# Pooling part of the second batch's pixels on GpSimd, and seventeen GELU chunks on VectorE

## The chip, the cores and the metric

The kernel runs on one core of one Trainium2 chip. A core has TensorE (PE in the profile; its weight loads are PEld), ScalarE (ACT), VectorE (DVE), GpSimd (POOL), SyncE (SP), and 16 DMA engines that all queues share. The metric is the device time of one execution in microseconds, lower is better; a few executions are taken and their median counts.

## The reference, cut to what matters

```python
# q: (4, 12288, 128)   kv: (4, 384, 32, 128)   w_sr: (128, 128)
kv_pool = kv.reshape(B, H // 4, 4, W // 4, 4, C).mean(axis=(2, 4))   # 96 x 8 pooled pixels
k = v = kv_pool.reshape(B, -1, C) @ w_sr                             # 768 keys for each batch
a = softmax(q @ k.T / sqrt(C));  x = (a @ v).reshape(B * S, D)       # 49152 x 128
h = x @ w_in;  out = (h / (1 + exp(-1.702 * h))) @ w_out             # w_in 128 x 2048, w_out 2048 x 128
```

Each batch's pixels are averaged over 4x4 blocks, projected to 768 keys that are also the values, and attended to by 12288 queries. The attention output goes through a two-layer network with a hidden width of 2048 and the quick GELU.

## The kernel before, in words

Queries are cut into 96 groups of 512, 24 to a batch; keys into six chunks of 128 (`JC`), the hidden width into 16 chunks of 128 (`FCH`). There are two rounds: attention of groups 0 to 47, their network, attention of groups 48 to 95, their network.

The unit of work is a **pass** of up to three chunks (`K = 3`). PE writes three 128x512 products into three PSUM banks (`fill_attn` at L347: keys times queries; `fill_moe` at L593: `w_in` times x), and one ACT instruction of 1536 columns takes exp (L349) or the GELU (L595) of them into a slot of `ag`. Two sets of three banks take turns, so PE fills one set while ACT reads the other. The first 30 passes are of one or two chunks. Later PE **drains** the slots: in attention twelve matmuls of 129 columns for three chunks (L360; the 129th column gives the sum for the division), in the network one matmul of 512 columns a chunk (L603). DVE divides (L383, L386) or transposes the result for the store (L614). `ag` has 102 slots, so that drains can lag behind fills.

Each engine executes its list in order. The lists are written by a **planner** in the kernel's Python (the loop at L794): it keeps a clock `now` in units of one 512-column matmul, believes ACT's pass to last `FIXED + CHUNK * 3` units, believes side jobs to last what `COST`, `COPY` and `RECIPROCAL` say, and decides which drain or side job goes on PE's list between two fills. Nothing of it runs on the chip: it changes only the order.

Some of ACT's work is done by DVE in about fifteen instructions a chunk: exp chunks (`early_exp`, from L428) and GELU chunks, the 16th chunk of chosen groups (`lent_gelu`, from L450, with two reciprocals at L470; its product is at L406). `lent` at L329 lists 14 of these: one in every third group from 52 on. The tile `aside` takes the results, three at a time.

**Pixels and keys.** Batches 0 and 1 are loaded in six chunks of 128 image rows by 16 pixels, cast to bf16 by the DMA that GpSimd issues (`load_chunk`, L130), into tiles of `x` that are not yet used. `pool_chunk` (L139) sums with 16 matmuls of 32 columns: the 128x32 matrix `sum4` adds four rows, four accumulated matmuls add four columns. DVE copies the pooled chunk (L142), and `key_and_value` (L161, L162) makes keys and values with two matmuls and two DVE copies. Batch 1's six loads are issued when the groups 10 and 12 begin, its jobs go into a list `extras` from group 15 on, one chunk a group; its keys are needed at group 24. Batches 2 and 3 are pooled by DMA accumulation and are not touched.

**Queries** beyond the first twelve groups are cast into `q_bf` in DRAM by GpSimd's queue (`cast_q`, L209) and come back transposed on SP's queue (`load_qT`, L215). `gate` (L517, L518) makes GpSimd's queue wait until DVE has come to a point of its list. `put_away` and `bring_back` (L500, L506) transpose the attention output through DRAM.

Of the kernel before, what the change touches and what calls it, by code (L numbers as in the profile page):

```python
# [7 lines left out]
F32 = mybir.dt.float32  # L8
F32R = mybir.dt.float32r
I32 = mybir.dt.int32  # L10
BF = mybir.dt.bfloat16
AF = mybir.ActivationFunctionType
AX = mybir.AxisListType
ADD = mybir.AluOpType.add
# [10 lines left out]
def kernel(  # L25
    ctx, tc, q, kv, w_sr, moe_w_in, moe_w_out, out,
):
    nc = tc.nc
    B, N, C = q.shape
    _, H, W, _ = kv.shape  # L30
    r = 4
    Hp, Wp = H // r, W // r
    J = Hp * Wp
    JC = J // 128
    d_ff = moe_w_in.shape[1]
    FCH = d_ff // 128
    scale = 1.0 / (C ** 0.5)
    G = 512
    SG = 4 * G
    NG = B * N // G  # L40
    NS = NG // 4
    GB = NG // B
# [10 lines left out]
    kv_r = kv.rearrange("b (ch p) (a w) c -> b a ch p (w c)", p=128, a=2)  # L53
# [6 lines left out]
    XS = NS // R  # L60
# [7 lines left out]
    kvtmp = ctx.enter_context(tc.tile_pool(name="kvtmp", bufs=1))  # L68
# [3 lines left out]
    opool = ctx.enter_context(tc.tile_pool(name="op", bufs=3))  # L72
# [8 lines left out]
    free = {2: 0.0, 5: 0.0, 6: 0.0, 7: 0.0}  # L81
    turns = [7, 6, 5]
    last_acc = 7

    def acc(key=None):

        nonlocal last_acc
        last_acc = next_acc()
        turns.append(last_acc)
        turns.remove(last_acc)  # L90
        if key:
            closes[last_acc] = key
        return banks[:, last_acc, :]

    def next_acc():
        return min((m for m in turns if m not in closes), key=lambda m: (max(free[m], now), turns.index(m)))
# [10 lines left out]
    now = 0.0  # L107

    x = xpool.tile([128, XS * SG], BF, name="x")
# [6 lines left out]
    HC = H // 128  # L116
    h = J // 2
    kv_tiles, kv_sums, pooled, pTs, kTs, vs = {}, {}, {}, {}, {}, {}

    def new_keys(b):  # L120
        kTs[b] = kvres.tile([128, J], BF, name="kT")

        vs[b] = kvres.tile([128, JC, C + 8], BF, name="v")
        nc.vector.memset(vs[b][:, :, C:C + 1], 1.0)

    def load_chunk(b, jc):

        a, ch = divmod(jc, HC)
        t = x_tile(XS - 1 - jc)
        nc.gpsimd.dma_start(out=t, in_=kv_r[b, a, ch])  # L130
        kv_tiles[b, jc] = t.rearrange("p (wp w1 c) -> p w1 wp c", w1=r, c=C)

    def pool_chunk(b, jc):
# [7 lines left out]
        pTs[b, jc] = kvtmp.tile([128, 128], BF, name="pTc", bufs=2)  # L141
        nc.vector.tensor_copy(pTs[b, jc], ps[:, 0:128])  # L142

    def key_chunk(b, jc):
        if jc == 0:
            new_keys(b)
        ps = acc()
        nc.tensor.matmul(ps[:, 0:128], w_sr_sb, pTs[b, jc], start=True, stop=True)
        nc.vector.tensor_copy(kTs[b][:, jc * 128:jc * 128 + 128], ps[:, 0:128])
# [5 lines left out]
        vs[b, jc] = True  # L155

    def key_and_value(b, jc):
        if (b, jc) == (1, 0):
            new_keys(b)
        ps = acc()  # L160
        nc.tensor.matmul(ps[:, 0:128], w_sr_sb, pTs[b, jc], start=True, stop=True)  # L161
        nc.tensor.matmul(ps[:, 128:256], pTs.pop((b, jc)), w_sr_sb, start=True, stop=True)  # L162
        nc.vector.tensor_copy(kTs[b][:, jc * 128:jc * 128 + 128], ps[:, 0:128])  # L163
        nc.vector.tensor_copy(vs[b][:, jc, 0:C], ps[:, 128:256])
        vs[b, jc] = True
# [52 lines left out]
    QS = 3  # L218
    qs = [x_tile(XS - 1 - JC - s) for s in range(QS)]

    def load_q(s, lo, hi):
        nc.gpsimd.dma_start(  # L222
            out=qs[s].rearrange("p (g e) -> p g e", g=4)[:, lo:hi, :],
            in_=q_flat[s * SG + lo * G:s * SG + hi * G, :].rearrange("(g p i) c -> p g (i c)", p=128, i=4))
# [22 lines left out]
    load_chunk(0, 1)  # L247
    load_q(0, 2, 4)
    load_q(1, 0, 2)
    for jc in range(2, JC):  # L250
        load_chunk(0, jc)
    load_q(1, 2, 4)
    for s in range(2, QS):
        load_q(s, 0, 2)
        load_q(s, 2, 4)
    cast_q(3)
    cast_q(4)

# [11 lines left out]
    for m in range(0, 128, 32):  # L270
        p = slice(m, m + 32)
        nc.vector.tensor_tensor(ident[p, p], row[p], col[p], EQ)
    sum4 = cpool.tile([128, 32], BF)
# [11 lines left out]
    w_sr_sb = cpool.tile([128, C], BF)  # L285
# [19 lines left out]
    parts = ag[:, 0:2 * SPLIT, :].rearrange("p (u a) t -> p u (a t)", a=2).bitcast(F32)  # L305
# [20 lines left out]

    early = range(NG // R, NG // R + EARLY)
    rolling = [(i, JC - 1) for i in [*range(38, NG // R, 6), *range(57, 90, 6)]]
    lent = [(g, FCH - 1) for g in range(52, 94, 3)]  # L329
    aside = agpool.tile([128, K, 512], BF, name="aside")  # L330

    def weights(c):
# [161 lines left out]
    PART, FIRST = 24, 3  # L494

    def put_away(n, m):
        size = PART // 2 if n == 0 and m > FIRST + 1 else PART
        for o in range(m * PART, m * PART + PART, size):
            lo = n * XS * SG + o * T
            nc.sync.dma_start(out=x_bf[lo:lo + size * T, :].rearrange("(k p) c -> p k c", p=T),  # L500
                              in_=x[:, o * T:(o + size) * T].rearrange("p (k c) -> p k c", k=size))
# [22 lines left out]
    def background(i):  # L524

        first_round = i < GB * 2
        s = TURN.get(i, NS) if first_round else i // 4 + 3 if i % 4 == 0 else NS
        if s < NS:
            load_qT(s)
        if i in CAST:  # L530
            gate()
            for s in CAST[i]:
                cast_q(s)
        if i in (10, 12):
            gate()
            for jc in range(i % 10 * 3 // 2, i % 10 * 3 // 2 + 3):
                load_chunk(1, jc)
        if 0 <= i - 16 < JC:
            extras.append((key_and_value, 1, i - 16))
        if 0 <= i - 15 < JC:  # L540
            extras.append((pool_chunk, 1, i - 15))
        if i in (28, 33, 38):
            put_away(0, (i - 28) // 5)
        if i in (31, 36, 41):
            bring_back(0, (i - 31) // 5)
        if i == 27:
            gate()
            nc.gpsimd.dma_start(out=w_in_sb, in_=moe_w_in)
        if i == 28:
            gate()  # L550
            nc.gpsimd.dma_start(out=w_out_sb, in_=moe_w_out.rearrange("(o p) c -> p o c", p=128))
# [34 lines left out]
    extras = []  # L586
# [67 lines left out]
    for n in range(R):  # L654
        part = [c for c in chunks if c[0] // (NG // R) == n]
        while part:
            m = sizes.pop(0) if sizes else K
            seq.append(("a", part[:m]))
            part = part[m:]
# [34 lines left out]
    def later(g):  # L694
        extras.append((transpose_q, g))

    def jobs(p):

        nonlocal now
        for f, *args in first.get(p, ()):  # L700
            if f in COST:
                now = max(now, free[next_acc()])
            f(*args)
            if f in COST:
                now += COST[f][0]
                free[last_acc] = copied(f)

    def prepare(p):

        nonlocal now  # L710
        kind, part = seq[p]
        for i, jc in part:
            if (kind, i) not in begun:
                begun.add((kind, i))
                (background if kind == "a" else background_moe)(i)
            while kind == "a" and ((key_and_value, i // GB, jc) in extras or (transpose_q, i) in extras):
                f, *args = extras.pop(0)
                now = max(now, free[next_acc()]) + COST[f][0]
                f(*args)
                free[last_acc] = copied(f)  # L720

    first = {
        0: [(pool_chunk, 0, 0), (transpose_q, 0), (warm, 1), (key_chunk, 0, 0), (transpose_q, 1)],
        1: [(value_chunk, 0, 0), (warm, 1)],
        2: [(pool_chunk, 0, 1), (warm, 2), (key_and_value, 0, 1), (warm, 1), (transpose_q, 2)],
        3: [(transpose_q, 3)],
        4: [(transpose_q, 4)],
        5: [(transpose_q, 5)],
# [6 lines left out]
        15: [(pool_chunk, 0, 5)],  # L735
        16: [(key_and_value, 0, 5), (later, 6)],
        17: [(later, 7)],
        18: [(later, g) for g in range(8, 12)]}

    FIXED, CHUNK, SWITCH, HANDOVER, EVACUATE = 0.295, 1.978, 6.0, 1.0, 4.5
    COST = {pool_chunk: (1.9, 2.6), key_chunk: (0.3, 2.4), value_chunk: (0.3, 2.4),
            transpose_q: (1.05, 4.2), early_fill: (1.0, 5.5), key_and_value: (0.55, 3.5),
            transpose_pooled: (0.9, 3.6), make_k: (0.8, 3.2), make_v: (0.8, 3.7)}
    COPY = {pool_chunk: 1.5, key_chunk: 1.5, value_chunk: 1.5, key_and_value: 2.8, transpose_q: 3.2}
    SMALL = 0.26
    RECIPROCAL = 10.5
    PAUSE = 4.0  # L750
    end, extra_at = [], 0.0
    source, dve = None, 0.0
# [7 lines left out]
    def copied(f):  # L760
        if f not in COPY:
            return now + COST[f][1]
        on_dve(COPY[f])
        return max(now + COST[f][1], dve)

    def fill(p):
        nonlocal now
        if p >= len(seq):
            return
        kind, part = seq[p]  # L770
        prepare(p)
        if p == 4:
            turns.insert(0, 2)
        if p == narrow - 5:
            for m in (2, 5):
                turns.remove(m)
        if p == narrow:
            assert not any(m in closes for m in (2, 5))
            now = max(now, free.pop(2), free.pop(5))
        lo = K * (p % 2)  # L780
        (fill_attn if kind == "a" else fill_moe)(part, banks[:, lo:lo + len(part), :])
        if p >= 2:
            now = max(now, end[p - 2] + HANDOVER / 2)
        now += len(part)
        begin = max(now + HANDOVER / 2, end[p - 1] if p else 0.0)
        if p and kind != seq[p - 1][0]:
            begin += SWITCH
        end.append(begin + FIXED + CHUNK * len(part))
# [101 lines left out]
```

The softmax here doesn't subtract the row's maximum and nothing guards it: scores larger than these inputs give would overflow.

## Time and profile before

| what | value |
|---|---|
| device time, median of 3 | 950.07 us (949.90 to 951.19) |
| span of the profiled execution | 948.6 us |
| PE busy | 941.8 us, 6314 matmuls |
| ACT busy | 934.9 us, 710 instructions |
| DVE busy | 536.5 us |
| GpSimd busy | 66.5 us |
| ACT passes of 1536 columns | 664 (502 GELU, 162 exp) |
| attention, first round | to 141.9 us |
| network, first round | to 487.3 us |
| attention, second round | to 604.3 us |
| network, second round | to the end |

An engine that is busy all the time need not be the one that sets the time: a matmul's record runs from its start to its modelled end, and matmuls overlap, so the starts of successive matmuls tell more than the busy share. ACT's instructions overlap too (1507 ns in the records of L595, while a new one starts about every 1340 ns).

### The profile page before, as it was taken

How to read it: one execution, taken by the hardware profiler on the slowest of the kernel's cores; microseconds unless marked ns; L12 is line 12 of the kernel's file. 1: busy time of each engine (PE TensorE's matmuls, PEld its weight loads, DVE VectorE, ACT ScalarE, POOL GpSimd, SP SyncE). 2: the span in 40 equal slices, each digit the busy share in tenths (PEclk: the TensorE clock that was granted, in tenths of full speed). 3: DMA queues.
4: the chain of work that ended last, by engine and by line, in shares of the span. 5: the costliest groups of instructions: out<-in, count | busy, mean ns of one | idle time of the engine just before them, and what ended most of it. 6: DMA issues, size and time to landing. Idle time of an engine off the chain costs nothing.

```text
span 948.6 us, 15423 instructions
## 1 busy us (share of the span) xinstructions
PE 941.8 (99%) x6314; PEld 502.9 (53%) x6314; DVE 536.5 (57%) x1035; ACT 934.9 (99%) x710; POOL 66.5 (7%) x114
## 2 busy tenths in 40 slices
PE   8999999999999999999999999999999999999998
PEld 4677776444444444454446777754444444444444
DVE  4643653102577777778655765365666665566631
ACT  6999999999999999999999999999999999999998
POOL 3101001320000232000000000000000000000000
PEclk9999999999999999999999999999999999999999
DMA  9999922999767799864335583562222222222222
GB/s 209 209 170 193 206 64 45 158 125 180 153 130 115 113 154 119 123 103 79 64 55 113 134 161 76 133 122 36 43 35 44 34 46 34 45 33 45 34 45 45
DMA packets 372855, 95.46 MB, mean 101 GB/s; under 512 B 346720, under 2 KB 370400, under 8 KB 372320
## 3 DMA queue, kind: packets, MB, share of 16 engines
q1 hardware_dynamic: 344000, 62.36, 36.9%
q0 software_dynamic: 28512, 31.99, 22.3%
q8 instruction: 49, 0.80, 0.4%
q14 instruction: 22, 0.18, 0.1%
q10 hardware_dynamic: 272, 0.13, 0.0%
HBM read 52.49 MB, written 48.76 MB: 107 GB/s over the span
## 4 chain that ended last, share of the span: by engine, by line
ACT 88%; PE 9%; DMA 2%; issue 0%; DVE 0%; POOL 0%; POOLq 0%
ACT ag L595 71%; ACT ag L349 17%; PE banks L347 4%; PE banks L360 3%; DMA qT<-q_bf 1%; DMA x<-in_kv_dram 1%; PE banks L139 0%; PE banks L593 0%; PE banks L631 0%; ACT L595 0%; PE banks L603 0%; PE banks L233 0%; ACT L349 0%; DVE kT L163 0%; POOL x L222 0%
## 5 line engine op out<-in xcount | busy, mean ns | idle before, releaser
L595 ACT ACTIVATE ag<-banks 128x1536 bf16<-128x1536 f32 (+1 forms) x510 | 682.2, 1507 | 0.0
L593 PE MATMUL banks<-x,w_in_sb 128*128 128x512 bf16 x1522 | 411.7, 379 | 0.1
L603 PE MATMUL banks<-ag,w_out_sb 128*128 128x512 bf16 x1506 | 407.8, 379 | 0.0
L349 ACT ACTIVATE ag<-banks 128x1536 bf16<-128x1536 f32 (+2 forms) x192 | 245.8, 1439 | 3.8 <-PE banks L347 3.4
L603 PEld LDWEIGHTS <-w_out_sb 128*128 128x128 bf16 x1520 | 148.4, 98 | 178.1 <-issue 0.9
L593 PEld LDWEIGHTS <-w_in_sb 128*128 128x128 bf16 x1522 | 147.3, 98 | 170.4 <-issue 1.1
L614 DVE STREAM_TRANSPOSE o_sb<-banks 128x512 f32<-128x512 f32 x95 | 67.9, 715 | 210.7 <-PE banks L603 195.0
L360 PEld LDWEIGHTS <-ag 128*128 128x128 bf16 x2272 | 146.1, 98 | 46.4 <-issue 0.6
L360 PE MATMUL banks<-v,ag 128*128 128x129 bf16 x2272 | 163.7, 220 | 0.1
L347 PE MATMUL banks<-qT,kT 128*128 128x512 bf16 x544 | 148.7, 379 | 1.6 <-DVE kT L163 1.0
L439 DVE SCALAR_TENSOR_TENSOR ea<-ea,eb 128x512 f32<-128x512 f32 x128 | 87.9, 687 | 3.2
L383 DVE RECIPROCAL rec<-banks 128x3 f32<-128x3 f32 x124 | 22.3, 180 | 95.9 <-PE banks L360 95.9
L386 DVE TENSOR_TENSOR x<-banks,rec 128x384 bf16<-128x384 f32 x124 | 69.1, 558 | 4.3
L347 PEld LDWEIGHTS <-kT 128*128 128x128 bf16 x544 | 46.3, 98 | 26.5 <-DVE kT L163 1.7
L470 DVE RECIPROCAL eb<-ea 128x256 f32<-128x256 f32 x28 | 47.6, 1727 | 0.5
L173 POOL DMA_DIRECT2D kvs<-in_kv_dram x32 | 40.4, 1299 | 17.8 <-DMA kvs<-in_kv_dram 15.2
L428 DVE TENSOR_SCALAR ea<-banks 128x512 f32<-128x512 f32 x32 | 22.1, 692 | 32.8 <-PE banks L412 32.5
L463 DVE SCALAR_TENSOR_TENSOR ea<-ea,eb 128x512 f32<-128x512 f32 x56 | 38.3, 685 | 1.6
L518 POOL MEMSET gate_tile<- 1x1 f32 x37 | 3.9, 105 | 326.6 <-DVE gate_tile L517 326.6
L434 DVE SCALAR_TENSOR_TENSOR eb<-eb,ea 128x512 f32<-128x512 f32 x32 | 22.1, 690 | 0.9
L450 DVE TENSOR_SCALAR qT<-banks 128x512 f32<-128x512 f32 x14 | 9.7, 692 | 17.2 <-PE banks L406 16.9
L441 DVE SCALAR_TENSOR_TENSOR ag<-ea,ee 128x512 bf16<-128x512 f32 x24 | 16.5, 688 | 0.7
(83 smaller groups left out, 267.9 us busy)
## 6 DMA issues: line engine op xcount, KB each, us to landing
out_dram<-o_sb SPq DMA_DIRECT2D x380, 64.0 KB, 2.0
kvs<-in_kv_dram POOLq DMA_DIRECT2D x32, 384.0 KB, 6.3
q_bf<-in_q_dram POOLq DMA_DIRECT2D x21, 512.0 KB, 6.9
x_bf<-x SPq DMA_DIRECT2D x13, 768.0 KB, 5.8
x<-in_kv_dram POOLq DMA_DIRECT2D x11, 512.0 KB, 10.4
x_bf<-x SPq DMA_DIRECT2D x6, 384.0 KB, 4.6
x<-in_q_dram POOLq DMA_DIRECT2D x5, 256.0 KB, 15.5
x<-in_kv_dram SPq DMA_DIRECT2D x1, 1024.0 KB, 5.1
```

The lines of the kernel that those rows point to most:

```text
L173: nc.gpsimd.dma_start(out=kv_sums[b][:, i2], in_=kv_p[b, i, w, :, i2], **({"accum_op": ADD} if n else {}))
L347: nc.tensor.matmul(ps[:, k, :], kTs[i // GB][:, jc * 128:(jc + 1) * 128], rhs, start=True, stop=True)
L349: nc.scalar.activation(place([("a",) + c for c in chunks]), ps, AF.Exp, scale=scale)
L360: nc.tensor.matmul(av_of[u][:, k * (C + 1):(k + 1) * (C + 1)], weights(("a", i, jc))[:, o:o + T], vs[i // GB][:, jc, 0:C + 1], start=(jc = ...
L386: nc.vector.tensor_tensor(to, ps[:, :, 0:C], rec.unsqueeze(2).broadcast_to([128, TS, C]), MUL)
L439: nc.vector.scalar_tensor_tensor(a, a, COEFFS[k], b, ADD, MUL)
L463: nc.vector.scalar_tensor_tensor(a, a, COEFFS[k], b, ADD, MUL)
L470: nc.vector.reciprocal(b[:, m:m + 256], a[:, m:m + 256])
L593: nc.tensor.matmul(ps[:, k, :], w_in_sb[:, fc * 128:(fc + 1) * 128], x[:, g % (4 * XS) * G:(g % (4 * XS) + 1) * G], start=True, stop=True)
L595: nc.scalar.activation(place([("m",) + c for c in chunks]), ps, AF.Gelu_apprx_sigmoid)
L603: nc.tensor.matmul(o_of[g], w_out_sb[:, fc, :], weights(("m", g, fc)), start=(fc == 0), stop=(fc == FCH - 1))
L614: nc.vector.transpose(o_sb, o_of.pop(g))
```

## The change

It has five parts.

1. Batch 1's chunks 0 to 3 are loaded as they are, in float32, on SP's queue (`load_pixels`, 1 MB each, two at a time into two halves of a region of `x`), and GpSimd adds their four columns in three additions of 512 elements a partition (`sum_pixels`), the last one into bf16. The loads of chunks 2 and 3 wait for the additions of chunks 0 and 1. Chunks 4 and 5 are still cast by loads of GpSimd's queue.
2. Batch 1's jobs take two chunks each: `pool_pair` (for summed chunks one matmul of 32 columns in place of four) with one DVE copy, then `key_pair` with one matmul of 256 columns, two of 128 and two DVE copies. They are put into `extras` at groups 17 to 22.
3. `lent` has 17 chunks, two in every five groups.
4. The planner's figures: arrival times of the first loads (`LAND`) and times at which a job's result is there (`ready`), `RECIPROCAL` 8.2 in place of 10.5, costs of the new jobs. One filler matmul (`warm`) of the start is left out.
5. `put_away` writes in halves from its second part on.

```diff
+    def load_pixels(jc):
+        a, ch = divmod(jc, HC)
+        o = (XS - 4 + jc % 2 * 2) * SG
+        t = x[:, o:o + 2 * SG].bitcast(F32)
...
+        nc.sync.dma_start(out=t, in_=kv_r[1, a, ch])
...
+    def sum_pixels(jc):
+        t = kv_tiles.pop((1, jc))
...
+        nc.gpsimd.tensor_tensor(t[:, 0], t[:, 0], t[:, 1], ADD)
+        nc.gpsimd.tensor_tensor(t[:, 2], t[:, 2], t[:, 3], ADD)
+        nc.gpsimd.tensor_tensor(sums[jc], t[:, 0], t[:, 2], ADD)
...
+    def pool_pair(b, jc):
+        ps = acc()
+        for k in range(2):
+            t = None if jc + k in sums else kv_tiles.pop((b, jc + k))
+            for wp in range(4):
+                o = k * 128 + 32 * wp
+                parts = [t[:, w, wp, :] for w in range(r)] if t is not None else [sums[jc + k][:, wp, :]]
+                for w, part in enumerate(parts):
+                    nc.tensor.matmul(ps[:, o:o + 32], part, sum4, start=(w == 0), stop=(w == len(parts) - 1))
...
+    def key_pair(b, jc):
...
+        nc.tensor.matmul(ps[:, 0:256], w_sr_sb, pT, start=True, stop=True)
+        for k in range(2):
+            nc.tensor.matmul(ps[:, 256 + k * 128:384 + k * 128], pT[:, k * 128:(k + 1) * 128], w_sr_sb,
...
-    lent = [(g, FCH - 1) for g in range(52, 94, 3)]
+    lent = [(g, FCH - 1) for g in range(52, 94) if g % 5 in (2, 4)]
...
-        size = PART // 2 if n == 0 and m > FIRST + 1 else PART
+        size = PART // 2 if n == 0 and m > 0 else PART
...
-        if i in (10, 12):
+        if i == 10:
             gate()
-            for jc in range(i % 10 * 3 // 2, i % 10 * 3 // 2 + 3):
+            for jc in range(2):
+                load_pixels(jc)
+            for jc in range(SUMS, JC):
                 load_chunk(1, jc)
-        if 0 <= i - 16 < JC:
-            extras.append((key_and_value, 1, i - 16))
-        if 0 <= i - 15 < JC:
-            extras.append((pool_chunk, 1, i - 15))
+        if 0 <= i - 11 < SUMS:
+            sum_pixels(i - 11)
+            if i - 9 < SUMS:
+                load_pixels(i - 9)
+        for at_, jc in ((17, 0), (19, 4), (21, 2)):
+            if i == at_:
+                extras.append((pool_sums if jc < SUMS else pool_pair, 1, jc))
+            if i == at_ + 1:
+                extras.append((key_pair, 1, jc))
...
-        2: [(pool_chunk, 0, 1), (warm, 2), (key_and_value, 0, 1), (warm, 1), (transpose_q, 2)],
+        2: [(pool_chunk, 0, 1), (warm, 2), (key_and_value, 0, 1), (transpose_q, 2)],
...
-    RECIPROCAL = 10.5
+    RECIPROCAL = 8.2
...
+        now = max(now, free[next_acc()], LAND.get((f, *args), 0.0), ready.get((f, *args), 0.0))
```

## The prediction

> **What bounds the kernel now.** The page's first part names two candidates, both at 99%:
>
> ```profile
> PE 941.8 (99%) x6314; PEld 502.9 (53%) x6314; DVE 536.5 (57%) x1035; ACT 934.9 (99%) x710; POOL 66.5 (7%) x114
> ```
>
> To part them I read the timeline of each by its starts, first PE in the second network round:
>
> ```profile
> 702.75 0.81 PE L593 MATMUL banks<-x,w_in_sb 128*128 128x512 bf16 x3
> 703.40 0.81 PE L603 MATMUL banks<-ag,w_out_sb 128*128 128x512 bf16 x3
> 704.05 0.81 PE L593 MATMUL banks<-x,w_in_sb 128*128 128x512 bf16 x3
> 704.70 0.38 PE L406 MATMUL banks<-x,w_in_sb 128*128 128x512 bf16 x1
> ```
>
> Three matmuls each 0.65 us, 0.2158 us for one, fills and drains alike, and no idle mark: no fill waits for ACT to release a bank. Now ACT, at 38 us and at 700 us:
>
> ```profile
> 38.65 12.20 ACT L349 ACTIVATE ag<-banks 128x1536 bf16<-128x1536 f32 x9
> ```
>
> ```profile
> 699.62 51.27 ACT L595 ACTIVATE ag<-banks 128x1536 bf16<-128x1536 f32 x38
> ```
>
> Without the last record (1.5 us), eight passes take 10.7 us, 1.333 each, the pace ACT can keep; 37 at 700 us take 49.8, 1.345 each. So ACT loses 12 ns a pass, some 8 us over 664 passes, while PE loses nothing. The table of PE's waits agrees; this is all of it, and the first and the kT, DMA x and ACT rows lie in the first 26 us:
>
> ```profile
> PE banks L347 <- DVE kT L163: 1.0, 4, 0.4
> PE banks L291 <- DVE col L263: 1.0, 1, 1.0
> PE banks L139 <- DMA x<-in_kv_dram: 0.5, 1, 0.5
> PE banks L412 <- DMA qT<-q_bf: 0.4, 1, 0.4
> PE banks L347 <- ACT ag L349: 0.2, 1, 0.2
> PE banks L347 <- DVE kT L149: 0.2, 1, 0.2
> ```
>
> I conclude that from 38 us on PE is the bound: its list has no holes, and the end is the time of 38 us plus the work on the list. The chain of waits gives ACT 88%, but it goes back along whichever engine has no gap, and ACT's overlapping records show none. Before 38 us ACT is the bound, as its passes of two chunks are dear:
>
> ```profile
> 32.30 0.59 PE L347 MATMUL banks<-qT,kT 128*128 128x512 bf16 x2
> 32.73 0.50 PE L360 MATMUL banks<-v,ag 128*128 128x129 bf16 x6
> 33.22 0.59 PE L347 MATMUL banks<-qT,kT 128*128 128x512 bf16 x2
> 33.65 0.50 PE L360 MATMUL banks<-v,ag 128*128 128x129 bf16 x6
> ```
>
> Here PE's two and six matmuls need 0.43 + 0.34 = 0.77 us, yet the next fill starts after 0.92: 0.15 us idle a pass.
>
> **What the Trainium skill says.** "TensorE: Matmul & The Clock Gate", section "Wait — 56ns, not 53.3ns?": warm matmuls start N/2.4 ns plus 2.5 apart, 215.7 ns at 512 columns, and never less than about 25 ns. The trace agrees (0.2158; 0.41/16 = 25.6 ns for L139, below). So PE is at its peak, not slowed. "GPSIMD Engine Reference", section "Performance versus the Vector engine": an addition of 2048 float32 takes 4497 ns; the trace of before has none. "SBUF — State Buffer", section "Who interferes with whom": a DVE instruction with two SBUF inputs and a GpSimd one that reads SBUF block each other; not seen before, but from 50 us on DVE's normal division (L386) reads PSUM, so I charge nothing.
>
> **The change part by part.**
>
> *Fewer pooling matmuls.* A job of 16:
>
> ```profile
> 52.10 0.55 PE L139 MATMUL banks<-sum,x 128*128 128x32 bf16 x16
> 52.51 0.81 PE L347 MATMUL banks<-qT,kT 128*128 128x512 bf16 x3
> ```
>
> 0.41 us. Batch 1 goes from 96 to 4 x 4 + 2 x 16 = 48 of them: -48 x 0.0255 = -1.22 us. Keys and values: twelve matmuls of 128 columns (0.056) become three of 256 (by N/2.4 + 2.5, 0.109) and six of 128: 0.67 against 0.66, nothing.
>
> *The start.* The order of the built kernel differs at the start by the filler, and in attention drains: when the fill of the 58th chunk has been listed, 75 matmuls of 129 columns have come before it, where it was 90. The 15 move from a stretch where PE idles to one where it does not: +15 x 0.0566 = +0.85 us. The filler (0.22 us) precedes a fill that waits for a key copy, of which 0.1 us could be won; but the pass at 17.14 us is fixed by the landing of the third pixel chunk (its pooling starts at 14.89 behind the DMA), so I count 0 to -0.1. The later keys hang on landings too (20.59). Time of the 58th chunk: -0.1 in all.
>
> Sum after the start: -1.22 + 0.85 = -0.37 us.
>
> *Three more chunks on DVE.* ACT has one pass fewer, 1.33 us. PE does the same fills and drains. By the above ACT was not the bound: zero. DVE gets 3 x 11.1 us (one chunk: L463 and its like eight times 0.69, five times 0.43, two reciprocals of 1.73, from the rows of part 5 and the timeline), on 193 us busy of 335 in that round: 68%. One in 17.7 us at the closest pace still fits between transposes. The order shows about 60 drain matmuls, 27 us, between the product of a lent chunk and its group's first drain, and the chunk takes about 14 us on DVE including interruptions: no wait.
>
> *Waits of the pooling jobs.* At 54.53 us PE idles 0.27 us behind L162 (starts of the timeline), I take it for a bank that frees late after crowded jobs; six jobs in place of twelve should remove it: -0.27.
>
> *The rolling exp at 100 us.*
>
> ```profile
> 99.26 0.50 PE L360 MATMUL banks<-v,ag 128*128 128x129 bf16 x6
> 100.12 0.39 PE L412 MATMUL banks<-qT,kT 128*128 128x512 bf16 x1 [0.36 <-DMA qT<-q_bf]
> ```
>
> L412 waits for a transposed load. In the new order these six drains stand behind it and not ahead, so PE gets there 0.34 us earlier and waits as much longer: +0.34. The load is issued at the same group.
>
> *GpSimd's sums, the new wait.* Loads of group 10 start at 38 us as before. The DMA engines are then busy with transposes until about 41 us. One cast chunk takes 10.4 us to land in company, the plain 1 MB 5.1 us alone:
>
> ```profile
> x<-in_kv_dram POOLq DMA_DIRECT2D x11, 512.0 KB, 10.4
> x<-in_kv_dram SPq DMA_DIRECT2D x1, 1024.0 KB, 5.1
> ```
>
> By the packet times a plain chunk costs the engines what a cast one does: both some 2.6 us of all 16. Four chunks then come in between 41 and 51: pixels 0 at about 46, pixels 1 at 51. Three additions are 3 x 1.12 = 3.4 us by the GpSimd page (estimate). Sum 0: 46.5 to 50; sum 1: 51.5 to 55. In the order the first job follows chunk 103, 57.7 us by the trace: 2.7 us to spare. Pixels 2 are loaded from 50, pixels 3 from 55, the latter behind a cast of queries, here at 62; sums end at 59 and 65.5; the job follows chunk 127, 68.2: again 2.7 us. What is queued behind: `cast_q` of queries 6 to 8 stands behind the sums and comes 8 to 18 us later than its 46.5 to 52.4, so the last is in by 73, and group 32 that needs it begins at 98. So zero; the other bound, additions of 2.2 us (twice the page), makes both jobs late by 3 to 6 us, and PE waits at the head of its list.
>
> Sum: -0.1 - 0.37 - 0.27 + 0.34 = -0.4 us, 949.7 us.
>
> **The rivals.** (a) ACT is the bound after all: then a pass fewer (1.33) and the ACT gaps beside the pooling jobs at 50.6, 54.8 and 58.9 us (0.46 above 1.331) count, -1.8 to -2.0: 948.2. For it: ACT's 99% and the chain. Against: 1.345 where it can do 1.333, and PE without holes. (b) GpSimd's sums come late: +2 to +6, 952 to 956. For it: margins of 2.7 us that hang on an unmeasured addition, and loads that wait for sums. Against: the page's price leaves the margins whole. (c) Lent chunks come too close and drains wait for DVE, +2 to +4: 953. For it: two in five groups, with the planner's reserve for reciprocals cut to what they take (8.2 units, 1.77 us, against 1.73). Against: the 27 us above.
>
> **How the numbers follow.** My forecast, near nothing, 0.58; (a) 0.22; (b) 0.16; (c) 0.04. The range takes in (a) and the near half of (b): 948.0 to 953.2. The 0.2% bound is 1.9 us, 948.17 and 951.97. (a) lies about on it, and some of the forecast's spread (removed waits up to 1 us) helps it: faster 0.22; slower, (b) and (c), 0.20; same 0.58.
>
> **What would show it.** In the profile after, PE from 150 to 930 us has starts 0.2158 us apart and no waits, and ACT in the last round runs at about 1.35 us a pass, slower than it could, with 245 passes of three. GpSimd's additions are near 1.1 us, and no row says that L176 waited for GpSimd. If ACT runs there at 1.333 and PE shows holes, step one was wrong; if PE waits for POOL at 57 or 68 us, the margins were; if the end moves over 1.5 us without a new wait, the account of the start or the worth of ACT's pass was.

## The result and the profile after

The changed kernel takes 956.65 us (median, 955.35 to 958.51) against 950.28 us (949.90 to 951.60) before: ratio 1.0066, interval 1.0053 to 1.0078. It is slower by 6.4 us, or 0.66%. The prediction was 949.7 us (948.0 to 953.2): it forecast next to no change, and the measured time lies above its whole range. The profiled execution took 955.35 us, the shortest of its kernel, with a span of 953.5 us against 948.6; the lines below account for these 4.9 us, and not for the 1.3 us by which the median lies higher.

The page's first part, kernel after:

```profile
PE 943.7 (99%) x6262; PEld 502.8 (53%) x6262; DVE 568.1 (60%) x1072; ACT 933.9 (98%) x709; POOL 79.0 (8%) x121
```

DVE and GpSimd took over what they were meant to (31.6 and 12.5 us more busy time) and ACT has one pass fewer. PE has the same 99%. The table of PE's waits, after:

```profile
PE banks L463 <- DMA qT<-q_bf: 2.8, 1, 2.8
PE banks L398 <- DVE kT L213: 1.0, 3, 0.4
PE banks L342 <- DVE col L314: 1.0, 1, 1.0
PE banks L139 <- DMA x<-in_kv_dram: 0.5, 1, 0.5
PE banks L689 <- DVE o_sb L672: 0.3, 1, 0.3
...
```

One row grew: L463 (L412 before) is the product of the exp chunk that DVE takes at 100 us. It waited 0.4 us for a transposed load of queries; now it waits 2.8. The wait at L689 is new; the two rows left out are of 0.2 us each and stood there before. No row names GpSimd, so the sums came in time in this execution. PE's timeline around that wait, after:

```profile
98.02 1.01 PE L411 MATMUL banks<-v,ag 128*128 128x129 bf16 x15
98.87 0.81 PE L398 MATMUL banks<-qT,kT 128*128 128x512 bf16 x3
102.53 0.61 PE L463 MATMUL banks<-qT,kT 128*128 128x512 bf16 x1 [2.84 <-DMA qT<-q_bf]
102.93 0.53 PE L411 MATMUL banks<-v,ag 128*128 128x129 bf16 x3
103.25 1.49 PE L398 MATMUL banks<-qT,kT 128*128 128x512 bf16 x3
104.53 1.18 PE L411 MATMUL banks<-v,ag 128*128 128x129 bf16 x9
105.51 0.87 PE L398 MATMUL banks<-qT,kT 128*128 128x512 bf16 x3
106.22 1.01 PE L411 MATMUL banks<-v,ag 128*128 128x129 bf16 x15
107.07 0.81 PE L398 MATMUL banks<-qT,kT 128*128 128x512 bf16 x3
```

Read the starts. Three matmuls at 98.87 take 0.65 us, so PE reaches L463 at 99.52 and idles 3.01 us (before, counted in the same way: at 99.60, 0.52 us). Then comes a second loss that no wait table shows. The three matmuls at 103.25 take until 104.53, 0.427 us each where 0.2158 is normal, and the nine of 129 columns 0.109 each where 0.0566 is normal: PE runs at half its clock until about 105.5. By these starts, counted from 102.53, the slow stretch costs 1.49 us. The page's row of the granted clock shows 9 in that slice, as the event is too short for it. Asked for the two stretches alone, the profile has it (the first figures are the length and PE's busy time, the third from the end is the granted clock):

```profile
98.81:102.22 3.41, 0.87 (x7) 0.26 (x4) 0.00 (x0) 2.44 (x2) 0.00 (x0) 1.00 1.25 126
102.22:105.63 3.41, 3.10 (x17) 2.01 (x18) 2.36 (x6) 0.86 (x1) 0.00 (x0) 0.50 1.21 245
```

Half the clock for 3.4 us lowers the mean of 953 us by 0.0018. The mean granted clock of all six executions is on record, 0.996 to 0.998, where 49 executions of the kernel before had 0.999 or 1.000. So by these means every execution of the changed kernel had such a stretch, and the one with 0.996 about two.

The load's issue on SP's queue, before and after:

```profile
92.36 5.04 SPq L215 DMA_TRANSPOSE qT<-q_bf  x1
97.44 3.31 SPq L506 DMA_TRANSPOSE x<-x_bf  x1
```

```profile
92.79 4.99 SPq L265 DMA_TRANSPOSE qT<-q_bf  x1
97.83 5.10 SPq L557 DMA_TRANSPOSE x<-x_bf  x1
```

Issued at 92.36 it landed at 100.12, 7.76 us later; issued at 92.79 it landed at 102.53, 9.74 us later. PE came 7.24 us after the issue before and 6.73 us after it now, because of the drains that moved behind the product. The longer wait is thus 0.51 us of order and 1.98 us of landing.

Starts of the same fills in both traces give the account:

| fill of chunk | before, us | after, us | difference | what lies between |
|---|---|---|---|---|
| 1 | 8.27 | 8.55 | +0.28 | first loads land later: scatter, 7.98 to 8.55 over all runs here |
| 59 | 37.80 | 38.08 | +0.28 | the start's new order: nothing |
| 180 | 92.02 | 92.28 | +0.26 | sums, pair jobs, moved drains: nothing net |
| 288 | 140.90 | 145.10 | +4.20 | wait +2.49, half clock +1.49 |
| 1313 | 603.34 | 607.45 | +4.11 | |
| 2000 | 912.43 | 916.60 | +4.17 | three more lent chunks: nothing |
| last matmul | 945.23 | 950.06 | +4.83 | end: +0.66, of it 0.44 more idle time |

The fills are counted without lent chunks, so the 2000th stands a little differently in the two lists: after, three more lent fills and four drains fewer come before it. The drains that come later are the other 0.22 us of the last row; of the idle time there, 0.47 us lie at L689 after and 0.10 at the same place before.

What else the prediction named can be read from GpSimd's timeline, after:

```profile
45.07 1.26 POOL L163 TENSOR_TENSOR x<-x 128x512 f32<-128x512 f32 x1 [4.96 <-DMA x<-in_kv_dram]
...
53.77 1.27 POOL L165 TENSOR_TENSOR o_sb<-x 128x512 bf16<-128x512 f32 x1
55.02 0.52 POOL L259 DMA_DIRECT2D q_bf<-in_q_dram  x1
59.43 0.52 POOL L259 DMA_DIRECT2D q_bf<-in_q_dram  x1
...
65.57 1.27 POOL L165 TENSOR_TENSOR o_sb<-x 128x512 bf16<-128x512 f32 x1
66.82 0.52 POOL L259 DMA_DIRECT2D q_bf<-in_q_dram  x1
79.40 0.98 POOL L259 DMA_DIRECT2D q_bf<-in_q_dram  x2
81.07 0.96 POOL L259 DMA_DIRECT2D q_bf<-in_q_dram  x2
85.06 0.55 POOL L606 DMA_DIRECT2D w_in_sb<-in_moe_w_in_dram  x1 [0.15 <-issue]
87.37 1.17 POOL L609 DMA_DIRECT2D w_out_sb<-in_moe_w_out_dram  x1 [0.15 <-issue]
```

Sums for the first pair end at 55.0 and for the second at 66.8. The three casts of queries 6 to 8 stand behind them, at 55.0, 59.4 and 66.8. Before:

```profile
46.72 0.51 POOL L209 DMA_DIRECT2D q_bf<-in_q_dram  x1
48.39 0.49 POOL L209 DMA_DIRECT2D q_bf<-in_q_dram  x1
52.37 0.49 POOL L209 DMA_DIRECT2D q_bf<-in_q_dram  x1
78.32 0.96 POOL L209 DMA_DIRECT2D q_bf<-in_q_dram  x2
82.31 0.96 POOL L209 DMA_DIRECT2D q_bf<-in_q_dram  x2
84.62 0.56 POOL L548 DMA_DIRECT2D w_in_sb<-in_moe_w_in_dram  x1 [0.15 <-issue]
86.29 1.17 POOL L551 DMA_DIRECT2D w_out_sb<-in_moe_w_out_dram  x1
```

The theory from here on: the late casts push the transposed loads of the same queries, then the casts of 9 to 12, `w_in` and `w_out` form one backlog on GpSimd's queue from 78 us on, and the load of queries 9, issued at 92 us on SP's queue, shares the engines with the packets of `w_out`. The backlog is the queue's and not that of full engines: before, from 78 to 92 us, the engines were under a tenth busy in 17 of 40 slices, with casts under way. Rivals: the order of PE's list is the cause; the sums themselves are; ACT is the bound after all. Two parts of the change can't have delayed this load, by their place: the writes in halves first appear at 105.41 us, and the lent chunks lie in the second round.

### The profile page after: what moved, and what is told of

Its sections match the earlier page's. It is cut to its first block, busy times and chain, and to the rows that moved or that the text cites. A ratio compares the mean times of both kernels' runs of the same rounds, so it can differ in the third digit from the quotient of the medians.

```text
span 953.5 us, 15381 instructions
## 1 busy us (share of the span) xinstructions
PE 943.7 (99%) x6262; PEld 502.8 (53%) x6262; DVE 568.1 (60%) x1072; ACT 933.9 (98%) x709; POOL 79.0 (8%) x121
## 4 chain that ended last, share of the span: by engine, by line
ACT 85%; PE 11%; DMA 3%; POOL 0%; issue 0%; DVE 0%; POOLq 0%
ACT ag L653 70%; ACT ag L400 14%; PE banks L398 5%; PE banks L411 4%; DMA x<-in_kv_dram 2%; DMA qT<-q_bf 1%; PE banks L651 0%; PE banks L661 0%; PE banks L689 0%; POOL x L272 0%; ACT L653 0%; POOL x L130 0%; ACT L400 0%; PE banks L176 0%; PE banks L463 0%
## 5 line engine op out<-in xcount | busy, mean ns | idle before, releaser
L661 PE MATMUL banks<-ag,w_out_sb 128*128 128x512 bf16 x1503 | 407.0, 379 | 0.0
L661 PEld LDWEIGHTS <-w_out_sb 128*128 128x128 bf16 x1520 | 148.4, 98 | 177.6 <-issue 0.7
L490 DVE SCALAR_TENSOR_TENSOR ea<-ea,eb 128x512 f32<-128x512 f32 x128 | 87.9, 687 | 3.8 <-DVE ea L490 0.6
L434 DVE RECIPROCAL rec<-banks 128x3 f32<-128x3 f32 x124 | 22.3, 180 | 98.7 <-PE banks L411 98.6
L398 PEld LDWEIGHTS <-kT 128*128 128x128 bf16 x544 | 46.7, 98 | 27.9 <-DVE kT L213 1.9
L521 DVE RECIPROCAL eb<-ea 128x256 f32<-128x256 f32 x34 | 57.7, 1724 | 0.5
L514 DVE SCALAR_TENSOR_TENSOR ea<-ea,eb 128x512 f32<-128x512 f32 x68 | 46.6, 686 | 2.0
L223 POOL DMA_DIRECT2D kvs<-in_kv_dram x32 | 40.5, 1293 | 21.6 <-DMA kvs<-in_kv_dram 17.9
L501 DVE TENSOR_SCALAR qT<-banks 128x512 f32<-128x512 f32 x17 | 11.8, 692 | 21.3 <-PE banks L457 21.2
```

The lines of the kernel that those rows point to most:

```text
L223: nc.gpsimd.dma_start(out=kv_sums[b][:, i2], in_=kv_p[b, i, w, :, i2], **({"accum_op": ADD} if n else {}))
L398: nc.tensor.matmul(ps[:, k, :], kTs[i // GB][:, jc * 128:(jc + 1) * 128], rhs, start=True, stop=True)
L490: nc.vector.scalar_tensor_tensor(a, a, COEFFS[k], b, ADD, MUL)
L514: nc.vector.scalar_tensor_tensor(a, a, COEFFS[k], b, ADD, MUL)
L521: nc.vector.reciprocal(b[:, m:m + 256], a[:, m:m + 256])
L661: nc.tensor.matmul(o_of[g], w_out_sb[:, fc, :], weights(("m", g, fc)), start=(fc == 0), stop=(fc == FCH - 1))
```

## The experiments

Each run is compared with the kernel before on the same chip (950.3 to 950.4 us).

### Which engine is the bound

**e4_act_less** makes ACT cheaper in the last network and leaves PE's list alone (the chunk not read goes through no GELU).

```diff
+        if len(chunks) == K and 50 <= chunks[0][0] < 94 and len(gelus) % 8 == 0:
+            to, ps = to[:, 0:2, :], ps[:, 0:2, :]
```

> The kernel before, where every eighth GELU pass of groups 50 to 93 in the second network round reads two chunks and not three, so that the GELU of about 28 chunks is left out; PE's list is the same. This takes about 28 x 0.43 = 12 us of work from ACT and nothing from PE. Theory (PE is the bound in the network): 949.5 to 950.5, no change. Rival (ACT is the bound): 938 to 942.

Measured 950.18 us, ratio 0.9998 (0.9990 to 1.0007), with ACT 7.4 us less busy (927.5; the expected 12 counts 28 chunks in full, and records that overlap are merged in the busy time). ACT's timeline in this run:

```profile
703.69 10.54 ACT L600 ACTIVATE ag<-banks 128x1536 bf16<-128x1536 f32 x8 [0.23 <-PE banks L594]
714.48 10.50 ACT L600 ACTIVATE ag<-banks 128x1536 bf16<-128x1536 f32 x8 [0.25 <-PE banks L594]
```

ACT now waits for PE once in eight passes: what it was relieved of became idle time.

**e9_pe_more** is the counterpart: 40 matmuls of 512 columns more in the first network (the first drain matmul of 40 groups done twice).

```diff
+        if fc == 0 and 4 <= g < 44:
+            nc.tensor.matmul(o_of[g], w_out_sb[:, fc, :], weights(("m", g, fc)), start=True, stop=True)
```

> The kernel before, in which the first drain matmul of each of the groups 4 to 43 in the first network round is done twice (the second overwrites the first): 40 x 0.2158 = 8.6 us more on PE, ACT untouched. Theory (PE is the bound): 958.9. Rival (ACT is the bound and PE has room beside it): under 954.

Measured 959.15 us against 950.42, ratio 1.0092 (1.0079 to 1.0106): +8.73 us, where 40 x 0.2158 is 8.63. Every matmul added is on the path. With e4, PE as the bound of the networks is shown for the kernel before, not argued.

**e5_lent17** puts the 17 lent chunks and their planner figure alone into the kernel before.

```diff
-    lent = [(g, FCH - 1) for g in range(52, 94, 3)]
+    lent = [(g, FCH - 1) for g in range(52, 94) if g % 5 in (2, 4)]
-    RECIPROCAL = 10.5
+    RECIPROCAL = 8.2
```

> The kernel before with only the 17 lent GELU chunks (and 8.2 for the planner's reciprocal): one ACT pass fewer, PE's work the same, the first 600 us untouched. Theory (PE is the bound): within 0.5 us of before, 949.8 to 950.8, or up to 0.5 more at the tail. Rival (an ACT pass is worth its 1.33 us): 948.9. Second rival (DVE comes late with 17): 952 or more and waits of L603 for DVE.

Measured 950.49 us, ratio 1.0004 (0.9997 to 1.0010). A pass less of ACT is worth nothing, and so is what DVE does more. The end of this run shows a wait of 0.3 us (L631, after DVE L614), as the changed kernel does at L689: part of its +0.66 at the end could come from here. But e7 below shows the same 0.3 us with 14 lent chunks, so this wait is not the lent chunks' alone.

### The load that PE waits for

**e2_w_late** moves the two weight loads of the changed kernel out of the stretch; the network needs them after 141 us only.

```diff
-        if i == 27:    # w_in
+        if i == 36:
-        if i == 28:    # w_out
+        if i == 38:
```

> The changed kernel, with the loads of the two network weights issued at groups 36 and 38 in place of 27 and 28. Theory (the load of queries at 93 us is late because the DMA engines still work on w_in and w_out): the wait at 99 us is gone or under 0.5 us, time 950 to 951.5. Rival (that load is slow by itself, from its collision with the transposes that bring back x, or from late casts): the wait stays at 2 us or more, 955 or more.

Measured 950.92 us, ratio 1.0007 (0.9998 to 1.0015): 5.7 us less than the changed kernel. The wait for the load is gone, and the half clock with it. What PE waits for in this run instead:

```profile
PE banks L176 <- POOL gate_tile L569: 1.3, 2, 0.9
```

L176 is the pooling job, and the row names the `gate` that stands right behind a sum in GpSimd's list. The sums came late here (their last casts at 58.5 and 69.8 in place of 55.0 and 66.8), so the margin that held in the changed kernel's profile doesn't always hold. This profile is of the longest of the 12 executions (952.37 us), so such a wait need not be the rule.

**e10_before_w_late** is the same edit in the kernel before.

> The kernel before with the network weights loaded at groups 36 and 38. Theory (the load at 93 us lands late because it shares the DMA engines with w_out, in the kernel before as well): the wait of 0.4 to 1.1 us at 99 us is gone, 949.3 to 949.9, the fastest of all here. Rival (that wait is made up elsewhere): 950.3.

Measured 949.84 us, ratio 0.9992 (0.9984 to 1.0000), the lowest of all runs. PE's timeline in it:

```profile
99.22 0.50 PE L360 MATMUL banks<-v,ag 128*128 128x129 bf16 x6
99.60 0.38 PE L412 MATMUL banks<-qT,kT 128*128 128x512 bf16 x1
```

PE reaches the product at 99.60 as before and the load is there. The load took 4.4 us from issue to landing, in place of 7.7. So the kernel before lost 0.5 us at this place and had no margin at all: any microsecond by which the load lands later was on the path.

**e6_casts_late** makes only the casts of queries 6 to 8 late in the kernel before. No sums, no new order.

```diff
-    CAST = {0: [5], 13: [6], 14: [7], 15: [8], 25: [9, 10], 26: [11, 12]}
+    CAST = {0: [5], 17: [6], 18: [7], 21: [8], 25: [9, 10], 26: [11, 12]}
```

> The kernel before with the casts of queries 6, 7 and 8 issued at groups 17, 18 and 21 in place of 13 to 15, about when the sums let them through in the changed kernel; nothing else. Theory (late casts push DMA work towards 93 us and delay the load that the rolling exp waits for, some 0.9 us of the 2 us that it lands later): the wait at 99 us grows from 0.4 to about 1.3 us, time about 951.2, no slow clock. Rival (lateness of casts is absorbed in the idle DMA time at 62 to 66 us): wait 0.4, 950.3.

Measured 954.72 us, ratio 1.0048 (1.0032 to 1.0064), +4.4 us (3.0 to 6.1) where 0.9 was expected, and with the slow clock that was not. PE's timeline in it:

```profile
99.14 0.50 PE L360 MATMUL banks<-v,ag 128*128 128x129 bf16 x6
102.09 0.39 PE L412 MATMUL banks<-qT,kT 128*128 128x512 bf16 x1 [2.45 <-DMA qT<-q_bf]
102.31 0.33 PE L360 MATMUL banks<-v,ag 128*128 128x129 bf16 x3
102.48 0.90 PE L347 MATMUL banks<-qT,kT 128*128 128x512 bf16 x3
103.18 1.50 PE L360 MATMUL banks<-v,ag 128*128 128x129 bf16 x12
```

The casts were issued at 57.1, 60.3 and 68.3; the load lands at 102.09, 1.97 us later than before, where the changed kernel had 2.41 (of it 0.43 a later issue). The half clock follows (1.30 us for twelve matmuls of 129 columns from 103.18 to the next start, where 0.68 is normal). Before and in e6, the weights stand behind the casts of 9 to 12 and are issued at the same moments (84.6 and 86.3; 84.5 and 86.2). Their us to landing, first before, then in e6:

```profile
w_out_sb<-in_moe_w_out_dram POOLq DMA_DIRECT2D x1, 512.0 KB, 12.2
```

```profile
w_out_sb<-in_moe_w_out_dram POOLq DMA_DIRECT2D x1, 512.0 KB, 15.2
```

`w_in` went from 10.2 to 11.5 in the same way, and the write of x on SP's queue was issued at 76.04 in place of 74.04. So the delay can be followed from transfer to transfer up to the load. Casts whose own data nobody needs before 98 us, delayed as in the changed kernel (1 to 2 us more), reproduce most of the loss.

**e3_no_sums** takes the other side: the changed kernel with all six chunks cast by loads, so that nothing stands ahead of the casts.

```diff
-    SUMS = 4
+    SUMS = 0
```

> The changed kernel with all six pixel chunks of batch 1 cast by loads at group 10, no additions on GpSimd; jobs of two chunks, 17 lent chunks and the planner's figures stay. Theory (the sums delay the casts of queries on GpSimd's queue, that backlog of DMA work reaches the load at 93 us): the casts are issued at about 46 to 53 us again, the wait at 99 us falls to 0.5 us or so, time 950 to 952 (pooling matmuls cost 1.2 us more). Rival (the wait comes from the order of the weights' gates and of the rolling exp, not from the sums): the wait stays 2 us or more, 956.

Measured 954.39 us, ratio 1.0045 (1.0030 to 1.0060). The theory in the form "the casts behind the sums are the whole cause" fell. The casts were back at 46.7, 48.4 and 52.4 us, yet PE's waits have

```profile
PE banks L463 <- DMA qT<-q_bf: 2.0, 1, 2.0
```

and the half clock after it (about 1.65 us). PE came to the product at 98.99 and the load landed at 101.12, an earlier coming and a later landing than before. But this profile is of the longest of four executions (956.12 us, mean clock 0.998); the other three took 954.10 to 954.64 at a mean clock of 1.000, so without the slow stretch. So the late casts suffice for the wait and the slow clock (four of e6's five executions have 0.998 or less); without them the rest of the change still costs about 4 us, mostly at full clock. Part of that lies elsewhere: the order of this list has PE idle for 0.6 us at 490 us too, where the changed kernel shows no such gap.

**e1_q9_early** issues the load of queries 9 earlier in the changed kernel.

```diff
-    TURN = {6: 3, 7: 4, 8: 5, 20: 6, 21: 7, 22: 8, 30: 9, 32: 10, 35: 11, 40: 12}
+    TURN = {6: 3, 7: 4, 8: 5, 20: 6, 21: 7, 22: 8, 28: 9, 32: 10, 35: 11, 40: 12}
```

> The changed kernel, with the transposed load of queries of groups 36 to 39 issued when group 28 begins and not at 30, so ahead of the 256-byte packets of w_out. Theory (late queries: PE waits 2.8 us for that load at 99 us, and its clock falls to half for about 1.5 us afterwards): the wait and the slow stretch are gone, time 950 to 951. Rival (other costs: the sums, the lent chunks or the tail carry most of the 6.4 us, and the wait at 99 us is but a place where lateness shows): 953 or more.

Measured 952.41 us, ratio 1.0022 (1.0013 to 1.0031). Issued at 86.89, 5.9 us earlier, the load landed at 100.78, only 1.75 us earlier, after 13.9 us. It is the backlog that sets the landing and not the issue. Packets of each queue from 95 to 99 us (q0 is GpSimd's queue with `w_out`, q1 is SP's with this load):

```profile
q0 software_dynamic: 1326, 0.34, 82.9%
q1 hardware_dynamic: 1328, 0.34, 64.3%
```

One packet of each in turn, 332 a microsecond; alone, in e2, the load moved 1132 in the microsecond from 96. The wait of 1.4 us is followed by matmuls at full clock, so of the theory the slow stretch went and half of the wait stayed.

### The order of PE's list

**e7_new_plan** gives the kernel before the new planner figures and the start without the filler; no transfer is changed.

```diff
+        now = max(now, free[next_acc()], LAND.get((f, *args), 0.0), ready.get((f, *args), 0.0))
-        2: [(pool_chunk, 0, 1), (warm, 2), (key_and_value, 0, 1), (warm, 1), (transpose_q, 2)],
+        2: [(pool_chunk, 0, 1), (warm, 2), (key_and_value, 0, 1), (transpose_q, 2)],
```

> The kernel before with only the planner's new figures for the start (arrival times, readiness, no filler): twelve old jobs, cast loads at groups 10 and 12, 14 lent chunks. The rolling exp then stands ahead of six drains and not behind them. Theory (the order alone brings PE to that exp about 0.7 us earlier, and the load lands later by the crowding of two cast pairs of queries): wait 1 to 2.2 us, with a slow clock if it is 2 or more; 951.5 to 954.5. Rival (only the new transfers make the load late): wait 1 us or less, 950 to 951.

Measured 952.48 us, ratio 1.0027 (1.0017 to 1.0036). The load was issued 1.1 us earlier than before and landed at 100.43, about as before, but PE came at 99.10: a wait of 1.2 us in place of 0.4. The rest of the +2.1 us is, by the working of the prediction, the 15 moved drains (0.85), and a wait of 0.3 us at the end that the trace shows. The new plan alone costs time.

**e12_old_plan** is the counterpart: the change's transfers, sums and jobs with the planner's old figures, the filler and 14 lent chunks.

```diff
-    LAND = {(transpose_q, 0): 0.9, (transpose_q, 1): 3.8, (pool_chunk, 0, 1): 15.1, ...}
+    LAND = {}
-    RECIPROCAL = 8.2
+    RECIPROCAL = 10.5
...
```

> The changed kernel with the planner's figures of before, the filler back and 14 lent chunks: of the change only the loads of pixels, the sums, the jobs of two chunks and the halves of the writes remain. Theory (late casts make the load at 93 us late by themselves, as they did in the kernel before): wait at 99 us 2 to 3 us and the slow clock, 954 to 956. Rival (it takes the new order too): 951 to 952.

Measured 955.37 us, ratio 1.0053 (1.0039 to 1.0067). PE came at 98.72, earlier than anywhere else, and the load landed at 103.58:

```profile
PE banks L463 <- DMA qT<-q_bf: 4.7, 1, 4.7
```

The wait is longer than the 2 to 3 us expected. The old figures don't rescue the change: its transfers make the load late in the old order too.

**e11_w_no_sums** is e2 without sums, so that the two differ in the 48 pooling matmuls, the sums and what follows from them in the planner's order.

```diff
-    SUMS = 4
+    SUMS = 0
```

> The changed kernel with late weights and with all six chunks of batch 1 cast by loads, so 48 pooling matmuls more on PE. Theory (PE is the bound there too, each matmul taken away is worth its 25 ns): 1.2 us over the kernel with late weights and sums, less what PE waits for the sums (up to 1.6 us), so 950.5 to 952. Rival (from 60 to 100 us PE waits for ACT now and then, the saving is lost there): 949.5 to 950.5, the sums only cost.

Measured 952.38 us, ratio 1.0021 (1.0012 to 1.0029), 1.46 us above e2, and each of the two intervals is 0.8 us wide to either side. This fits a saving of 1.22 us, but does not measure it: in e11's profile PE waits 0.4 us for DVE at L661, which e2's doesn't, and e2's has the 1.3 us of waits for the sums.

**e8_w_jobs_late** tries to keep the saving: weights late, and the summed pairs' jobs later so that PE doesn't wait for them.

```diff
-        for at_, jc in ((17, 0), (19, 4), (21, 2)):
+        for at_, jc in ((18, 4), (20, 0), (22, 2)):
```

> The changed kernel with the network weights loaded at groups 36 and 38, and the pooling jobs put off: the pair of cast chunks first at group 18, the summed pairs at 20 and 22. Theory (beside the wait at 99 us, PE waits up to 1.6 us for GpSimd's sums, in some executions): both waits gone, 949.3 to 950.3, at or under before. Rival (the sums are not waited for outside that one profile): the same as with late weights alone, 950.9.

Measured 950.69 us, ratio 1.0012 (1.0000 to 1.0025). No wait for the load or for the sums is left, and it is still not below the kernel before: the rival's figure. The order is that of e7, whose 15 moved drains (0.85) and wait at the end (0.3) would take back about what the sums save; this is a sum of terms and not a run.

**e13_sums_old_plan_w_late** goes one step further and takes the old planner figures and 14 lent chunks as well.

> The pixels' loads, GpSimd sums and jobs of two chunks with the planner's figures of before, 14 lent chunks, the network weights loaded at groups 36 and 38, the jobs at groups 18, 20 and 22. Theory (each pooling matmul saved is worth its 25 ns on PE, nothing else differs from the kernel before with late weights at 949.84): 48 fewer, -1.2 us, less what is waited for: 948.6 to 949.2, the fastest. Rival (waits for sums or for key copies eat it): 949.6 to 951.

Measured 950.71 us (949.78 to 953.92), ratio 1.0002 (0.9994 to 1.0011). The load makes PE wait 1.0 us again, without the weights. Here it stood behind the write of x on SP's queue, which was issued at 78.7 us and took 17.9 us to land beside the casts. Between 62 and 75 us PE idles some 0.8 us, 0.15 at a time, most likely behind ACT. The rival that gave the saving away was right. Six of the 13 executions took 949.78 to 949.97 us; even these are no faster than e10, which has no sums. No version with the sums beat the kernel before; the only one that may is e10, without them.

### The same load in all of them

PE's coming is read from the starts; the landing is the start of the product where PE waits for it, and the issue plus the profile's time to landing where not. The wait is the trace's. The last column counts the executions whose mean granted clock is 0.998 or less, wherever the slow stretch lay, so that the profiled one isn't taken for all.

| run | casts 6 to 8, us | `w_out`, us | load issued | landed | took | PE came | wait | half clock in the profile | executions with it |
|---|---|---|---|---|---|---|---|---|---|
| before | 46.7 to 52.4 | 86.3 | 92.4 | 100.1 | 7.7 | 99.6 | 0.4 | no | 0 of 49 |
| e5 | 46.5 to 52.1 | 86.1 | 92.1 | 100.6 | 8.4 | 99.4 | 1.1 | no | 1 of 20 |
| e7 | 46.5 to 52.2 | 87.5 | 91.2 | 100.4 | 9.2 | 99.1 | 1.2 | no | 1 of 9 |
| e3 | 46.7 to 52.4 | 86.2 | 92.3 | 101.1 | 8.8 | 99.0 | 2.0 | yes | 1 of 4 |
| e6 | 57.1 to 68.3 | 86.2 | 92.2 | 102.1 | 9.8 | 99.5 | 2.4 | yes | 4 of 5 |
| after | 55.0 to 66.8 | 87.4 | 92.8 | 102.5 | 9.7 | 99.5 | 2.8 | yes | 6 of 6 |
| e12 | 56.5 to 67.8 | 86.7 | 92.2 | 103.6 | 11.4 | 98.7 | 4.7 | yes | 4 of 4 |
| e1 | 56.8 to 68.0 | 87.1 | 86.9 | 100.8 | 13.9 | 99.3 | 1.4 | no | 0 of 12 |
| e10 | 46.7 to 52.3 | late | 92.3 | 96.7 | 4.4 | 99.6 | 0 | no | 0 of 13 |
| e11 | 46.6 to 52.2 | late | 92.1 | 97.9 | 5.7 | 98.9 | 0 | no | 0 of 13 |
| e2 | 58.5 to 69.8 | late | 94.0 | 98.5 | 4.5 | 100.7 | 0 | no | 0 of 12 |
| e8 | 55.8 to 67.0 | late | 91.9 | 96.0 | 4.2 | 99.8 | 0 | no | 2 of 22 |
| e13 | 57.8 to 70.6 | late | 92.7 | 100.1 | 7.4 | 98.9 | 1.0 | no | 1 of 13 |

With `w_out` in the stretch and early casts the load takes 7.7 to 9.2 us, with `w_out` and late casts 9.7 to 11.4. Without `w_out` it takes 4.2 to 5.7 with early casts and with late ones, but for e13. That fits two streams sharing the engines, as the Trainium skill has it in "DMA: Bandwidth & Descriptors", section "Queues, rings and completion order": an engine takes a packet of each queue in turn, so a transfer slows down as long as another queue has work. The traces agree: 1326 packets of one queue beside 1328 of the other in e1, and loads that land in 3.7 us at the least and 4.3 in the median, but in 7.7 to 13.9 us beside the 256-byte packets of `w_out`. Before and e5 have the same transfers and the same list up to there, so single profiles differ by some 0.5 us in the landing.

## Why the prediction was wrong

**The bound: right.** PE was the bound before (e4, e9). For the kernel after, the starts say the same. In the last network 40 of ACT's passes take

```profile
702.53 53.93 ACT L653 ACTIVATE ag<-banks 128x1536 bf16<-128x1536 f32 x40
```

(53.93 - 1.5) / 39 = 1.344 us a pass, not the 1.333 it can keep, and PE's starts are 0.2158 apart, as foretold:

```profile
702.28 0.81 PE L661 MATMUL banks<-ag,w_out_sb 128*128 128x512 bf16 x3
702.92 0.81 PE L651 MATMUL banks<-x,w_in_sb 128*128 128x512 bf16 x3
```

So rival (a) was wrong, and "a pass fewer" is worth zero (e5; +4.11 to +4.17 in the account).

**The pooling matmuls**, -1.22, fit the runs (1.46 between e11 and e2), but no run measured them alone. **The moved drains**, +0.85, fit e7, but were not run by themselves. **Waits of the pooling jobs**, -0.27, came out with the other sign: the wait at 54.53 us is gone, but by the starts PE's idle time between 50 and 75 us grew from 0.40 to 0.93 us, some 0.15 at a time. No row of the waits names what for; ACT is the likely one. This takes back what the two terms before it leave, so that fills 59 to 180 take as long as they did.

**The sums' own lateness: a thin margin, not the cause.** The additions take 1.26 us; my estimate from "GPSIMD Engine Reference", section "Performance versus the Vector engine", was 1.12. They ended 2.4 and 1.6 us ahead of their jobs (57.5 and 68.4) in the profile of after, where the prediction had 2.7 for both. In e2's profile PE waited 1.3 us for them.

**The first step that failed** was "What is queued behind: `cast_q` of queries 6 to 8 ... the last is in by 73, and group 32 that needs it begins at 98. So zero." It asked who reads the delayed casts and stopped there. It should have asked which transfers follow them on the same queue and on shared engines. e6 puts a number on it: about the same delay without anything else costs 4.4 us, where the prediction has zero.

**The second** was "The rolling exp at 100 us: ... +0.34", with "The load is issued at the same group" as its reason for leaving the landing alone. The profile before showed a load that landed 0.5 us too late, with several transfers queued from 78 us on, so its landing had no margin. The order's part was about right (0.51 in place of 0.34); the landing, taken as fixed, cost 1.98.

**Two terms were not in the sum at all:** the half clock after the wait, 1.49 us, and the end, +0.66 us (0.44 of it idle), where the last group's drains now come wholly behind the fills and PE waits for DVE once. +0.28 at the first fill is scatter. The account is 0.28 + 2.49 + 1.49 + 0.66 = 4.9 us, of the 4.9 of the spans. Rival (b) named the right side and nearly the size, 952 to 956, but as a wait for the sums; the wait was further down the queue. Seen from the runs: late casts alone cost 4.4 us (e6), the new order alone 2.1 (e7), the lent chunks 0.2, within noise (e5). From the changed kernel, late weights take away 5.7 us (e2). These don't add up term by term, as most of them act on the same wait.

**Open.** Why in e3, with early casts, the load still lands 1.0 us later than before is not settled: its casts of 9 to 12 were issued at 78.9 and 80.5 in place of 78.3 and 82.3, I have not run that alone, and half of that delay is within the scatter of single profiles. Why e13 has a wait that e2 and e8 don't have, with casts as late, is read from one trace only. The other executions of after, up to 958.51, have no trace: their clocks show the slow stretch, a longer wait is likely, not shown.

## What to carry to other kernels

When an edit delays a transfer, follow the queue and the engines it shares to the next load that something waits for, and not only the delayed data's reader. A wait of a few tenths of a microsecond in the profile before is not a small cost but a sign of no margin: each later landing there counts in full. Where PE is the bound, count what its clock does after a wait as well as the wait.

## What was not expected of the hardware

The clock fell after waits that I should have thought harmless. By "TensorE: Matmul & The Clock Gate", section "What's actually happening", the clock goes to half after an idle window of about 3.4 us. Here waits of 1.0, 1.1, 1.2 and 1.4 us (e13, e5, e7, e1) were followed by full speed, and waits of 2.0, 2.4, 2.8 and 4.7 us (e3, e6, after, e12) each by half speed, at a cost of about 1.5 to 1.9 us. In all four the granted clock was 0.50 for 3.41 us, whatever the wait. In the 3.41 us just before, PE had been busy for 1.44, 0.99, 0.87 and 0.00 us in the same order. So a stretch that was not wholly idle was enough here, and where the page's sentence reads otherwise, the measurement decides. The slow one began 0.7 and 1.0 us after the end of the wait in e3 and e6, and 0.3 and 0.4 us before it in after and e12. Four and four waits in one place of one kernel are few; the bound lies between 1.4 and 2.0 us of waiting here, and where the stretches fall may move it.
